# A one-core attention-and-MLP kernel with a written-out order: planner rates corrected and the order searched anew

## The chip, the cores and the metric

The kernel runs on one core of one Trainium2 chip. The engines that work here are TensorE (PE; its weight loads have a row of their own, PEld), VectorE (DVE), ScalarE (ACT), GpSimd (POOL) and SyncE (SP); DMA queues move data between HBM and the on-chip memories. The metric is the device time of one execution in microseconds (us), as the median of several runs. All times in the profile count from the first instruction of the profiled execution.

## The reference

The reference is a Nyström attention over 8 batches of 8 heads (576 tokens, head size 64, 32 landmarks), followed by a two-layer MLP with a squared ReLU on the 4608 tokens (model width 512, inner width 2048):

```python
q_lm = q.reshape(B, H, 32, 18, D).mean(axis=3); k_lm = likewise
A  = softmax(scale * q @ k_lm.T)      # 576 x 32 per head
Bm = softmax(scale * q_lm @ k_lm.T)   # 32 x 32
C  = softmax(scale * q_lm @ k.T)      # 32 x 576
Z  = Bm.T / (norm1(Bm) * norminf(Bm) + 1e-6)
for _ in range(6): Z = 2 * Z - Z @ Bm @ Z
x  = A @ Z @ C @ v                    # heads side by side: 4608 x 512
out = (relu(x @ w_in) ** 2) @ w_out
```

## The kernel before

The kernel never forms x. For each batch b it computes a matrix WP = Z C v w_in (128 x 2048 for each half of the heads), so that the first MLP layer is A·WP, and then relu, square and w_out.

Every piece of work is an `op` with a name, a table of engines that may run it with a planned duration for each, what it reads and writes, and a function that emits its instructions. An order written out by hand as one long string, `ORDER`, lists all 1437 ops. Each word is `name@banks/engine`: `@` gives the PSUM banks, `/A`, `/D`, `/P` choose ACT, DVE or POOL, and without a suffix the first engine of the op's table runs it. `Plan.schedule` walks the string once with the planned durations and transfer rates, gives each op a planned start, sorts by it, and the instructions are emitted in that order. So the string fixes, for each engine, a queue that is worked strictly from front to back: an instruction that waits holds up all that stand behind it on its engine.

The names, with b the batch:

- `ldk/ldq{b}.{r}`, `ldv{b}.{r}{i}`, `win{ch}{r}`, `wout{i}`: loads, all issued from POOL's DMA queue (fp32 in HBM, bf16 on chip). Two words that begin with `lx`: for batches 3 to 5 a second load of q or k into the tile `XS` for the landmarks (`load_xs`). `la{b}.{t}{j}`: for batches 6 and 7 three loads per operand (t = 0 is q, 1 is k), of which j = 1 and 2 *add* into the fp32 tile that j = 0 filled; that tile lies in `XS`, and each of the three waits for the one before it (`load_sums`, issued at line 443).
- Landmarks: `lm` (PE; batches 3 to 5 read `XS` at line 500), `lma` (line 510) and `lmc` (line 514) finish the sums of batches 6 and 7 in fp32 on DVE or POOL, `lme` scales, `lmt` transposes. `T{b}.{t}{r}`: DVE transposes of k and q.
- The 32 x 32 softmax: `B`, `Bmx`, `Bsb`, `Bex`, `Bsu`, `Brc`, `Bml`, and the norms `Bcs`, `Bnm`, `Bad` (line 670), `Brn`. The six steps of Z: `N{b}.{i}` on PE, `U{b}.{i}` on DVE, and from batch 2 on `bd{b}.{i}` (line 679, DVE or POOL) between them.
- The other softmaxes: `SS` or `SC`/`SA` on PE; `Cmx`, `Cex`, `Crc`, `Cnr` (line 422), `CT`; `At`, `Amx`, `Asb`, `Aex`, `Asu`, `Arc`, `Aml` (line 1081, in batches 0 and 1 line 1026), `Ap`, `Ab`.
- The product: `CV`, `CVe`, `Zm` (line 898), `ZC` (line 911, in batch 0 line 908), `ZCe`, `W` (line 935), `We`.
- The MLP: `F` (A·WP, four matmuls at line 1111), `R` (relu out of PSUM, ACT line 1132 or DVE line 1134), `Q` (square, ACT line 1139, DVE or POOL line 1141), `O` (w_out, four quarters of four matmuls each at line 1158 for each of 36 token tiles), `Oe` (copy out of PSUM), `St` (store, from SP's queue).

In the order the MLP of batch b stands between the small attention ops of batches b+1 and b+2, and `O` quarters fill PE where an attention chain would leave it waiting.

The planner counts two things that matter here. Ops that name DVE and POOL in `port=` are planned one after the other, as users of one port that the two engines share. A transfer lands after the bytes queued ahead of it, at a rate that depends on the planned time:

```python
sw = max(sw, free[e] + 0.5)
sw += o.nbytes / RATE["first" if sw < 23.0 else "then" if sw < 48.0 else "late"]
o.end, o.kind = sw + LAND, ""
```

The planned times set nothing on the chip except the order; on the chip an instruction starts when its semaphores and its engine allow it. A few short filler matmuls (line 1236) keep PE going in the first 22 us.

Of the kernel before, what the change touches and what calls it, by code (L numbers as in the profile page):

```python
# [265 lines left out]
def kernel(  # L266
# [207 lines left out]
    def attention(b):  # L474
# [32 lines left out]
        def landmarks_added():  # L507
            acc, ls, kS = ACC[i2], LS[:, 0, 0:256].rearrange("p (t r d) -> p t r d", t=2, d=D), ("LS", 0)
            for t in range(2):
                op(f"lma{b}.{t}", {"POOL": 0.9, "DVE": v_(384)}, lambda e, t=t: eng(e).tensor_tensor(  # L510
                    acc[:, t, :, 0:3], acc[:, t, :, 0:3], acc[:, t, :, 3:6], ALU.add),
                   R=[("ACC", i2, t)], W=[("ACC", i2, t)], port=("POOL", "DVE"))
# [765 lines left out]
c17 c0 ldk0.1 c1 ldq0.1 ldq0.0 ldk0.0 ldq1.0 ldk1.0 c2 ldk1.1 c12 c3 c5 ldq1.1 c6 c15 c13 ldv0.10  # L1278
T0.11 c10 c11 ldv0.11 lm0.1@0 c8 T0.01 lmc0.10/D ldv0.00 lmc0.11/D lme0.1 c9/A lmt0.1 T0.00
SC0.1@4 win31 lm0.0@1 Cmx0.1 T0.10 lme0.0 Cex0.1 lmt0.0 T1.00 bk0/P B0@6 c14/A Bmx0 SC0.0@4 Bsb0  # L1280
CT0.1 Bex0 win30 Bsu0 SA0.0@0 Brc0 Cmx0.0 Bml0/P Bce0@2 win10 Bmb0/A Bcs0 Btr0 Cex0.0 Amx0.0b
BBT0@3 Bnm0 Asb0.0b SA0.1@6 Brn0 CT0.0 Aex0.0b Zi0/P Yi0 win11 Amx0.0a N0.0@1 Amx0.1a lm1.0@5
win01 U0.0 Asu0.0b win00 N0.1@4 Asb0.0a lm1.0a U0.1 Aex0.0a ldv1.11 Amx0.1b N0.2@2 Arc0.0b
# [7 lines left out]
F0.12@4 R0.16 ldv1.00 F0.14@6 Zi1 Q0.22 c18 F0.10@2 Q0.18 R0.14 O1.0@1 Btr1 Q0.20 R0.10 ldv1.10
Q0.14 R0.12 F0.26@6 Q0.16 Aex1.0 F0.8@2 Q0.10 F0.30@4 R0.26/D R0.8 O0.0@0 T1.10 R0.30 ldq3.0
Q0.12/A F0.24@2 Asu1.0 Aex1.1 F0.28@6 T1.11 BBT1@4 lx3.1 R0.28 O1.1 Yi1 Asu1.1 Q0.8/A Q0.30/P
N1.0@5 O0.1 R0.24 U1.0 T2.10 ldk3.0 Q0.24/A N1.1@5 SC1.0@6,2 Q0.26 U1.1 O3.0@4 Cmx1.1 Arc1.0
N1.2@5 Cex1.1 O3.1 Aml1.0/P U1.2 Cmx1.0 N1.3@5 lm2.0@2 ldv3.11 U1.3 Q0.28 ldq3.1 Arc1.1 N1.4@5
Aml1.1/P lmc2.00 O1.2 U1.4 lmc2.01 Cex1.0 lme2.0 O0.2 lmt2.0 T2.00 lx3.0 B2@2 N1.5@5 O1.3 Bmx2
U1.5 Crc1 Bsb2 CT1.0 Bex2 O3.2 ldq5.0 Bsu2 Cmk1 Oe1.0 Brc2 CT1.1 Bml2 Ap1.1@6 St1 Btf2 ldk3.1
Btr2/A Bcs2 Zd1@3 CR1@1 Bct2 Ab1.1/A O3.3 bt2/D Bnm2 Bad2 CRe1 Brn2 T2.11 BBT2@5 Zi2/P CV1@6,1
Oe3.0 ldv2.10 Zm1 St3 O0.3 Yi2 CVe1.1/A CVe1.0 bd2.0 T2.01 ZC1@7 Ap1.0@2 Oe0.0/D ZCe1.0 N2.0@1
O2.0@4 Ab1.0/A ZCe1.1/D St0 U2.0 ldk4.1 bd2.1/D W1.2@5 W1.0@0 W1.1@2 We1.00 We1.01/D N2.1@7 O2.1  # L1300
We1.1 ldk5.0 U2.1 We1.2/D W1.3@0 ldv3.10 O2.2 We1.3 bd2.2 T3.00 F1.4@2 F1.0@6 R1.4/D F1.2@0 R1.0
N2.2@5 O2.3 Q1.4 R1.2 U2.2 bd2.3/D Q1.0/A F1.8@2 T3.10 Oe2.0 N2.3@7 F1.12@0 U2.3 F1.6@5 R1.8/D
St2 R1.12 lm3.0@4 bd2.4/D R1.6 Q1.12 Q1.2 F1.20@0 lme3.0 lx4.0 Q1.6 N2.4@6 lmt3.0 F1.10@2 R1.20
U2.4 ldv2.00 F1.14@4 T3.01 R1.10 B3@6 bd2.5 O5.0@0 R1.14 Bmx3 Bsb3 lx4.1 T3.11 Q1.10/A N2.5@3
SS2.0@6,1,4 Q1.20/A U2.5 ldq5.1 Q1.8 O5.1 At2.0 Q1.14/A ldv2.11 O5.2 Bex3 Bsu3 ldv3.00 Brc3
Amx2.0 SS2.1@4 O5.3 Bml3 Cmx2.1 ldq4.0 At2.1 O4.0@3 Cex2.1 Cmx2.0 O4.1 Oe5.0 ldk6.1 Asb2.0 Cex2.0
St5 F1.16@4 Zm2.2 Btf3 F1.18@1 Aex2.0 Bcs3 Amx2.1 F1.22@6 R1.16 O4.2 Asb2.1 R1.22 Q1.16/A F1.28@4
Q1.22 Bct3 F1.30@6 R1.18 R1.28/D O4.3 R1.30 Btr3 Crc2.0 Asu2.0 bt3 Q1.18/A F1.24@1 ldq6.0 Bnm3
F1.26@6 Bad3 R1.24 Brn3 Arc2.0 ldv4.00 O6.0@4 R1.26 Q1.24 Aml2.0 BBT3@5 Oe4.0 O6.1 ldv4.10 Aex2.1
Yi3 Q1.26 SS3.0@2,0,6 Q1.30/A Asu2.1 lm4.0@5 Zi3/P Q1.28/A At3.0 O6.2 Cnr2.0/A lx5.1 Crc2.1  # L1310
Arc2.1 Cnr2.1 lme4.0 O6.3 lx5.0 CT2.1 CT2.0 SS3.1@6 ldk5.1 Aml2.1 Oe6.0 O7.0@5 Cmx3.1 St6 bd3.0
O7.1 Cmx3.0 Cex3.1 At3.1 N3.0@4 O7.2 Cex3.0 U3.0 Zm2.1 lmt4.0 CV2@6,0 Ab2.1 bd3.1 Amx3.1 B4@2
ldk4.0 CVe2.0/A O7.3 Zm2.0 CVe2.1/A Crc3.1 Zm2.3 ldq4.1 Cnr3.1/A Bmx4 Ab2.0 N3.1@7 ZC2@4 O8.0@6
# [6 lines left out]
Zm3.0 R2.11 Arc3.1 O10.0@1 Q2.4 Q2.14/A Aml3.1 O10.1 R2.8 Asu3.0 Q2.8/A F2.15@2 lmt5.0 Arc3.0  # L1320
Q2.11/A CV3@4,6 Aml3.0 O9.1 Q2.13 CVe3.0/A CVe3.1/A Zm3.1 Ab3.0 R2.15 F2.12@4 T5.01 la6.10 ZC3@6
O9.2 R2.12 Q2.15 ZCe3.0/D Btr4/A la6.01 Q2.12/A O10.2 ZCe3.1/D bt4/D Bcs4 T4.00 W3.3@6 ldv6.11
W3.0@2 Ab3.1 W3.2@4 We3.0 We3.3/D O9.3 We3.2 O10.3 Oe9.0/D la7.10 BBT4@6 Bct4 F3.0@2 Oe10.0 Bnm4
F3.1@4 Bad4 Brn4 R3.0 T4.11 St10 Zi4/P O12.0@7 la7.01 R3.1 Yi4 bd4.0/D F3.2@0 T4.01 Q3.1/A St9
N4.0@6 W3.1@2 R3.2 U4.0 B5@4 O12.1 bd4.1/D We3.1 Bmx5 T5.00 N4.1@6 F3.3@0 Bsb5 Q3.2/A U4.1 O12.2
bd4.2 Bex5 R3.3/D Q3.0/A F3.6@4 Bsu5 la6.02 Brc5 T4.10 F3.5@0 N4.2@6 F3.4@2 Q3.3 R3.5 U4.2 la6.11
O12.3 R3.6 bd4.3/D Q3.5 R3.4 Bml5 N4.3@6 F3.9@0 Btf5 U4.3 Oe12.0 F3.7@4 Bcs5 bd4.4 R3.9/D F3.13@2
St12 la7.11 Bct5 F3.10@6 Q3.9/A R3.7/D N4.4@0 O11.0@1 R3.13 Q3.6 U4.4 R3.10 Bnm5 O11.1 T5.10
bd4.5 Q3.4/A SS4.0@2,4,6 Q3.7 Q3.10/A Bad5 N4.5@0 O11.2 la7.02 Brn5 Btr5 U4.5 At4.0 O11.3 bt5
Amx4.0 SS4.1@6 Zi5/P Oe11.0 ldv4.11 O13.0@0 Cmx4.1 St11 Cmx4.0 O15.0@1 Cex4.1 At4.1 O15.1 Cex4.0  # L1330
Asb4.0 BBT5@6 F3.12@4 Zm4.0 Aex4.0 Yi5 F3.11@2 Zm4.3 Crc4.1 Amx4.1 F3.8@6 R3.11 la6.12 Asu4.0
# [80 lines left out]
```

## Time and profile before

| What | Value |
|---|---|
| Median of 3 runs (lowest, highest) | 259.1 us (259.07, 259.11) |
| The profiled execution's own time | 259.34 us |
| Its span, first to last instruction | 257.6 us |
| Granted TensorE clock, mean | 0.999 |
| Busy: PE, DVE, ACT, POOL | 247.5, 212.5, 175.6, 85.1 us |
| Instructions | 7492 |
| HBM read, written | 48.50 MB, 9.44 MB |

In the profile a row of the timeline or of the chain gives a start, a length, the engine, the line of the source, the operation with its output and inputs, and a count. A bracket at the end of a timeline row is the time that the engine sat idle before it and what ended that idleness. A PE row's length runs to the modelled end of its last matmul, while the next group may start before that end, so a busy share of 96% doesn't say that PE runs at its peak; starts are compared with starts below. Rows of the 32 x 32 work and of POOL are rougher than the others.

### The profile page before, as it was taken

How to read it: one execution, taken by the hardware profiler on the slowest of the kernel's cores; microseconds unless marked ns; L12 is line 12 of the kernel's file. 1: busy time of each engine (PE TensorE's matmuls, PEld its weight loads, DVE VectorE, ACT ScalarE, POOL GpSimd, SP SyncE). 2: the span in 40 equal slices, each digit the busy share in tenths (PEclk: the TensorE clock that was granted, in tenths of full speed). 3: DMA queues.
4: the chain of work that ended last, by engine and by line, in shares of the span. 5: the costliest groups of instructions: out<-in, count | busy, mean ns of one | idle time of the engine just before them, and what ended most of it. 6: DMA issues, size and time to landing. Idle time of an engine off the chain costs nothing.

```text
span 257.6 us, 7492 instructions
## 1 busy us (share of the span) xinstructions
PE 247.5 (96%) x3043; PEld 138.1 (54%) x3043; DVE 212.5 (82%) x553; ACT 175.6 (68%) x324; POOL 85.1 (33%) x137
## 2 busy tenths in 40 slices
...
GB/s 99 209 190 204 206 209 207 208 240 227 224 225 209 223 230 283 164 194 181 196 138 205 192 156 94 3 80 46 43 21 104 43 42 0 3 124 42 10 67 129
DMA packets 24610, 36.53 MB, mean 142 GB/s; under 512 B 2560, under 2 KB 13632, under 8 KB 24576
## 3 DMA queue, kind: packets, MB, share of 16 engines
...
q1 hardware_dynamic: 5760, 9.31, 14.0%
q8 instruction: 24, 0.39, 0.6%
q10 hardware_dynamic: 160, 0.13, 0.2%
...
HBM read 48.50 MB, written 9.44 MB: 225 GB/s over the span
## 4 chain that ended last, share of the span: by engine, by line
PE 66%; DMA 15%; DVE 10%; POOL 3%; issue 2%; ACT 2%; DVEq 0%; POOLq 0%
PE ps L1158 38%; PE ps L1111 16%; DMA X<-in_q_dram 9%; DMA XS<-in_q_dram 6%; PE ps L935 3%; DVE RS L1134 2%; PE ps L864 2%; DVE G L1141 2%; POOL X L429 1%; PE ps L778 1%; ACT WP L416 1%; DVE sm L816 1%; PE ps L529 1%; PE ps L742 1%; DVE An L1081 1%
## 5 line engine op out<-in xcount | busy, mean ns | idle before, releaser
L1158 PE MATMUL ps<-w_out,G 128*128 128x512 bf16 (+1 forms) x592 | 138.3, 374 | 0.3 <-DVE RS L1134 0.3
L1158 PEld LDWEIGHTS <-G 128*128 128x128 bf16 x592 | 53.2, 98 | 53.9 <-issue 6.0
L1111 PE MATMUL ps<-AT,WP 128*128 128x288 bf16 (+2 forms) x512 | 71.2, 286 | 1.1 <-DVE RS L1134 0.8
L1132 ACT ACTIVATE RS<-ps 128x576 bf16<-128x576 f32 (+2 forms) x101 | 61.1, 651 | 10.5 <-PE ps L1111 5.0
L1111 PEld LDWEIGHTS <-WP 128*128 128x128 bf16 x512 | 48.5, 98 | 20.6 <-issue 2.5
L1139 ACT ACTIVATE G<-RS 128x576 bf16<-128x576 bf16 (+2 forms) x55 | 36.4, 686 | 2.1 <-DVE RS L1134 1.8
L416 ACT COPY OS<-ps 128x512 f32<-128x512 f32 (+1 forms) x32 | 18.3, 573 | 23.0 <-PE ps L1158 21.8
L1141 DVE TENSOR_TENSOR G<-RS 128x576 bf16<-128x576 bf16 (+2 forms) x71 | 30.1, 445 | 2.6 <-ACT RS L1132 2.0
L416 ACT CAST WP<-ps 128x1024 bf16<-128x1024 f32 (+1 forms) x25 | 23.5, 983 | 6.7 <-PE ps L935 6.5
L679 POOL TENSOR_TENSOR BD<-ST,blkb 128x256 bf16<-128x256 bf16 x15 | 10.8, 718 | 47.4 <-DVE ST L756 43.2
L1134 DVE TENSOR_SCALAR RS<-ps 128x576 bf16<-128x576 f32 (+2 forms) x27 | 20.4, 760 | 4.9 <-PE ps L1111 3.8
L484 DVE STREAM_TRANSPOSE TT<-X 128x576 uint32<-128x576 uint32 x32 | 24.3, 761 | 0.0
L819 ACT ACTIVATE C<-ps,sm 128x576 bf16<-128x576 f32 x16 | 14.2, 902 | 7.7 <-DVE sm L816 7.7
L756 DVE SCALAR_TENSOR_TENSOR ST<-ST,ps 128x128 bf16<-128x128 bf16 (+1 forms) x48 | 12.8, 266 | 5.9 <-PE ps L742 3.6
L455 POOL DMA_DIRECT2D V<-in_v_dram x24 | 14.5, 603 | 6.2 <-DMA X<-in_q_dram 2.6
L420 DVE COPY OS<-ps 128x512 f32<-128x512 f32 x5 | 3.4, 675 | 12.3 <-PE ps L1158 12.3
L816 DVE TENSOR_REDUCE sm<-ps 128x1 f32<-128x576 f32 x16 | 11.5, 747 | 1.2 <-PE ps L778 1.1
L1236 PE MATMUL ps<-onesb 128*128 128x512 bf16 (+1 forms) x36 | 10.6, 392 | 1.6 <-DVE onesb L352 1.6
L420 DVE CAST WP<-ps 128x1024 bf16<-128x1024 f32 (+1 forms) x9 | 9.9, 1100 | 1.8 <-PE ps L935 1.7
L429 POOL DMA_DIRECT2D X<-in_q_dram x16 | 9.8, 642 | 4.1 <-PE ps L1111 2.2
L429 POOL DMA_DIRECT2D X<-in_k_dram x16 | 9.7, 607 | 3.6 <-DMA X<-in_k_dram 1.3
L1081 DVE TENSOR_TENSOR An<-SA,smA 128x640 bf16<-128x640 f32 (+1 forms) x12 | 10.3, 864 | 0.1
...
## 6 DMA issues: line engine op xcount, KB each, us to landing
...
X<-in_q_dram POOLq DMA_DIRECT2D x16, 288.0 KB, 11.0
...
XS<-in_q_dram POOLq DMA_DIRECT2D x6, 384.0 KB, 6.5
XS<-in_k_dram POOLq DMA_DIRECT2D x6, 384.0 KB, 7.1
...
```

Source lines behind the costliest of these rows:

```text
L416: nc.scalar.copy(o, i)
L429: lambda e: nc.gpsimd.dma_start(x[:, t, r].rearrange("p s d -> p (s d)"), src),
L455: lambda e, r=r, p0=p0, n=n, src=src: nc.gpsimd.dma_start(vv[32 * p0:32 * (p0 + n), r].rearrange("p s d -> p (s d)"), src),
L484: op(f"T{b}.{t}{r}", {"DVE": v_(576) + 0.02}, lambda e, r=r: nc.vector.transpose(tt[:, t, r].rearrange("p s m e -> p (s m e)").bitcast(U32 ...
L816: op(f"Cmx{b}.{r}", {"DVE": v_(576)}, lambda e, r=r: nc.vector.tensor_reduce(s_[:, 12 + r:13 + r], cbanks(r), axis=AX.XY, op=ALU.max, nega ...
L819: op(f"Cex{b}.{r}", {"ACT": a_(576) + 0.27}, lambda e, r=r: nc.scalar.activation(Cs[r][:].rearrange("p x u -> p u x"), cbanks(r), AF.Exp, ...
L1111: nc.tensor.matmul(ps[:, ph.at + i, 0:w], lhsT=wp[:, r, 128 * ff:128 * ff + 128], rhs=at[:, r, t0:t0 + w], start=(r == 0), stop=(r == 1))
L1132: nc.scalar.activation(rs, pair(ph, w), AF.Relu)
L1134: nc.vector.tensor_scalar(out=rs, in0=pair(ph, w), scalar1=0.0, scalar2=None, op0=ALU.max)
L1139: nc.scalar.activation(g, rs, AF.Square)
L1141: eng(e).tensor_tensor(g, rs, rs, ALU.mult)
L1158: nc.tensor.matmul(bank(po)[:, 0:c1 - c0], lhsT=G[:, f, lo:lo + P], rhs=w_out[:, f, c0:c1], start=(f == 0), stop=(f == NF - 1))
```

## The change

Four planner constants are corrected: the rate of late loads goes from 0.385 to 0.355 MB/us, the counted size of an adding load from 1.5 to 0.5 of 786,432 bytes, and POOL's planned durations for the fp32 additions from 0.9 to 1.5 us (`lma`) and from 0.65 to 1.0 us (`lmc`). None of the four is seen by the chip. `ORDER` is replaced as a whole: the same 1437 ops, each emitted as before, in another order, with other PSUM banks, and 164 of them on another engine: 67 go from DVE to ACT, 62 from ACT to DVE, 20 from POOL to DVE, 14 from DVE to POOL and one from POOL to ACT. PE's ops, the loads and the stores keep their engines.

```diff
-RATE = {"sw": 0.375e6, "hw": 0.2e6, "first": 0.385e6, "then": 0.4e6, "late": 0.385e6}
+RATE = {"sw": 0.375e6, "hw": 0.2e6, "first": 0.385e6, "then": 0.4e6, "late": 0.355e6}
...
-                op(f"lma{b}.{t}", {"POOL": 0.9, "DVE": v_(384)}, lambda e, t=t: eng(e).tensor_tensor(
+                op(f"lma{b}.{t}", {"POOL": 1.5, "DVE": v_(384)}, lambda e, t=t: eng(e).tensor_tensor(
...
-                op(f"lmc{b}.0{j}", {"DVE": v_(256), "POOL": 0.65}, lambda e, j=j: eng(e).tensor_tensor(
+                op(f"lmc{b}.0{j}", {"DVE": v_(256), "POOL": 1.0}, lambda e, j=j: eng(e).tensor_tensor(
...
-ADD_COST = 1.5
+ADD_COST = 0.5
```

The order, at the places that the prediction speaks of. The end of batch 0's attention and the first `F`:

```diff
-N0.3@2 win20 lme1.0 U0.3 Cmk0 CVe0.1/A lmt1.0 CVe0.0/A N0.4@6 Aml0.0a/P T1.01 CR0@5 B1@0 CRe0/A
-wout0 U0.4 Bmx1 bk1 N0.5@4 Bsb1 Ap0.0@5 U0.5 Asu0.1a ldq2.1 Zd0@3 Ab0.0/A SA1.0@0 Zm0 Bex1
-Arc0.1b Bsu1 Aml0.1b/P ZC0@2 Brc1 Amx1.0 SA1.1@6 ZCe0 c7 Arc0.1a Bml1/P Asb1.0 Aml0.1a/P W0.1@2
-Amx1.1 W0.3@4 wout1 We0.1 Ap0.1@0 Bmb1 Asb1.1 ldk2.1 We0.3 ldk2.0 F0.6@2 Ab0.1 W0.0@6 Blo1/P R0.6
...
-R0.20/D R0.2 F0.18@4 R0.0 Q0.2 W0.2@6 Bad1 F0.22@2 R0.18/D We0.2 Q0.0/P F0.16@0 Brn1 R0.22/D
...
+CT0.0 c7 N0.1@1 Asb0.0a lm1.0a U0.1 Aex0.0a Amx0.1b N0.2@0 Asu0.0a lm1.0b U0.2 Arc0.0a T1.01
+Aml0.0a/P N0.3@4 lme1.0 CV0@5,0 U0.3 win31 Asb0.1b N0.4@7 lmt1.0 Aex0.1b win30 Crc0 U0.4 CVe0.0/A
+Cmk0 Asu0.1b CVe0.1/A N0.5@7 bk1/P CR0@5 U0.5 Amx0.1a CRe0/A Zd0@6 Asu0.0b wout0 Arc0.1b Arc0.0b
+Zm0 SA1.0@4 Aml0.0b wout1 Asb0.1a ZC0@7 Ap0.0@5 Amx1.0 ZCe0 ldk2.0 Aex0.1a W0.0@0 Ab0.0/A Asu0.1a
+ldq2.0 We0.00 W0.1@2 Arc0.1a We0.01/D Aml0.1b/P SA1.1@6 We0.1 Asb1.0 Aml0.1a/P B1@0 Amx1.1 Aex1.0
+F0.4@2 ldk2.1 Ap0.1@4 Bmx1 ldq2.1 R0.4 Bsb1 Asb1.1 Bex1 F0.2@0 Ab0.1/A Q0.4 W0.2@2 R0.2/D F0.6@6
+We0.2 F0.20@4 Bsu1 Q0.2/P R0.6/D F0.0@0 R0.20 W0.3@2 wout2 R0.0/D F0.18@6 We0.3 Q0.20 F0.22@4
```

The adding loads of batches 6 and 7, and what stands around them:

```diff
-lm5.0@1 R2.9 Q2.0 Q2.6/A N3.4@0 F2.4@6 Q2.9 la6.00 U3.4 F2.13@4 R2.10 bd3.5/D CT3.0 O9.0@0 lme5.0
...
-ldv6.00 Q3.15/A N5.2@6 ldq7.1 CV4@2,4 Zm4.2 O14.3 CVe4.0/A CVe4.1 Ab4.0 ZC4@2 U5.2 O15.3 Oe14.0
-bd5.3/D Aml4.1 ZCe4.0 N5.3@3 O13.3 Oe15.0 ZCe4.1/D U5.3 T5.11 St15 W4.0@6 Oe13.0 W4.1@1 Ab4.1
-O16.0@3 We4.1 bd5.4/D T6.00 St13 lma7.0 O16.1 We4.0 lma6.0/D W4.2@1 St14 W4.3@4 We4.2/D F4.0@6
...
+lm5.0@4 R2.5 St6 Q2.0 Q2.5/A R2.6/D N3.4@5 F2.9@0 la7.00 lme5.0 F2.7@2 U3.4 R2.9 St7 bd3.5/D
+F2.8@6 Bsu4 lmt5.0 Q2.6/A la6.00 Asb3.0 N3.5@5 F2.4@0 R2.7 O10.0@4 Brc4 Bml4 R2.4 U3.5 Zm3.0
...
+Q2.11/A Q2.10 CT3.1 B5@6 R2.13 F2.14@0 la7.01 Bmx5 Btr4 Bsb5 O9.1 Q2.8/A T4.01 Aex3.0 Bcs4 bt4
+CV3@2,6 Bct4 R2.14 Bnm4 la6.01 Asu3.0 O9.2 CVe3.0/A CVe3.1/A Bad4 Brn4 Q2.14/A Zm3.2 F2.15@2
+Aml3.1 ldq5.1 ZC3@0 F2.12@6 la6.10 T4.10 R2.15 O10.1 ZCe3.0 Arc3.0 Q2.15/A ZCe3.1/D Q2.13 O10.2
+R2.12 Aml3.0 Q2.12/A W3.2@2 Ab3.1 W3.0@6 Bex5 W3.3@0 We3.2/D la6.02 We3.0 O9.3 We3.3 O10.3 Ab3.0
+ldq4.0 T4.11 la7.10 BBT4@6 Oe9.0 F3.3@2 Oe10.0/D O12.0@7 R3.3 Yi4 St10 Zi4/P la7.02 Q3.3/A W3.1@0
+bd4.0/D F3.1@5 T5.10 We3.1 St9 N4.0@4 O12.1 ldq7.1 lma6.0/D R3.1 la6.11 U4.0 Bsu5 Q3.1/A Brc5
+bd4.1/D F3.0@3 F3.2@0 ldv6.11 T4.00 R3.0 N4.1@2 F3.6@5 R3.2 U4.1 O12.2 bd4.2/D Q3.0/A Q3.2 N4.2@4
...
+W4.2@6 ldq7.0 Aml4.0 W4.0@4 O16.0@1 We4.0 Ab4.1 Ab4.0 O16.1 We4.1 lma7.0/D We4.2/D F4.0@4 lme6.0
+lma7.1 O16.2 R4.0 lmt6.0 T6.11 O16.3 lmc7.00/P N5.5@0 lmc7.01/P SS5.0@6,4,2 Oe16.0 U5.5 Q4.0/A
```

Of the ops that move between engines, by kind: 17 `R` and 25 `Q` go from DVE to ACT, 21 `R` and 18 `Q` from ACT to DVE; of POOL's, `lma7.0`, `bd7.4`, nine more `bd`, `bt3`, `bt5` and seven other small ones go to DVE, and `Q0.0` to ACT; to POOL go `bk1`, `Q0.2`, `lmc7.01`, six `bd`, `bt4` and four other small ones. The second load of `XS` for batch 5 (`lx5.0`) has 33.31 MB of loads up to and with it in POOL's queue in place of 34.78 MB (fp32 bytes, an adding load with its real 0.39 MB; `ldk6.1`, `ldq6.0` and others go behind it, `ldk6.0` and others ahead), and `la6.00` 36.31 in place of 37.54 MB.

171 lines of the change are left out of this document (81 added, 90 removed).

## The prediction

> **What bounds the kernel now.** I read the page first, then the chain, then PE's timeline wherever PE sat idle, then the engines that it had waited for, last the loads.
>
> ```profile
> span 257.6 us, 7492 instructions
> PE 247.5 (96%) x3043; PEld 138.1 (54%) x3043; DVE 212.5 (82%) x553; ACT 175.6 (68%) x324; POOL 85.1 (33%) x137
> ...
> PE 66%; DMA 15%; DVE 10%; POOL 3%; issue 2%; ACT 2%; DVEq 0%; POOLq 0%
> ...
> L1132 ACT ACTIVATE RS<-ps 128x576 bf16<-128x576 f32 (+2 forms) x101 | 61.1, 651 | 10.5 <-PE ps L1111 5.0
> ...
> L1139 ACT ACTIVATE G<-RS 128x576 bf16<-128x576 bf16 (+2 forms) x55 | 36.4, 686 | 2.1 <-DVE RS L1134 1.8
> ...
> L1141 DVE TENSOR_TENSOR G<-RS 128x576 bf16<-128x576 bf16 (+2 forms) x71 | 30.1, 445 | 2.6 <-ACT RS L1132 2.0
> ...
> L1134 DVE TENSOR_SCALAR RS<-ps 128x576 bf16<-128x576 f32 (+2 forms) x27 | 20.4, 760 | 4.9 <-PE ps L1111 3.8
> ```
>
> PE is the bound: it carries most of the chain, and no other engine is near its span. The chain in order of time gives the two phases and the length of dense groups.
>
> ```profile
> 16.83 0.81 PE ps L529 x6
> ...
> 24.13 0.44 DVE ZM L890
> ...
> 24.82 0.47 issue
> ...
> 52.67 0.97 PE ps L1158 x4
> 53.75 0.49 PE ps L1037 x4
> 54.30 0.86 PE ps L1158 x4
> ...
> 99.31 0.49 PE ps L1111 x4
> ```
>
> Up to the first `F` the chain changes engine at each step; later it is nearly all PE. A quarter of `O` takes 0.86 when its like follows and 0.97 when another shape of matmul does, so a change of shape costs about 0.1 us. PE's timeline shows the first `F`, the stalls behind it, and the place of `N4.0`:
>
> ```profile
> 27.84 0.61 PE L1111 MATMUL ps<-AT,WP 128*128 128x256 bf16 x4 [0.21 <-ACT WP L416]
> ...
> 33.73 1.03 PE L1111 MATMUL ps<-AT,WP 128*128 128x256 bf16 x8 [0.83 <-DVE RS L1134]
> ...
> 96.46 0.73 PE L500 MATMUL ps<-XS,seg 96*32 96x256 bf16 x20 [0.75 <-DMA XS<-in_q_dram]
> ...
> 111.95 0.23 PE L742 MATMUL ps<-ST,BD 128*128 128x64 bf16 x2
> ...
> 135.25 1.04 PE L1158 MATMUL ps<-w_out,G 128*128 128x512 bf16 x4
> 136.45 0.22 PE L911 MATMUL ps<-ZM,CV 128*128 128x64 bf16 x2 [0.17 <-DVE ZM L898]
> 136.91 0.23 PE L911 MATMUL ps<-ZM,CV 128*128 128x64 bf16 x2 [0.24 <-DVE CV L420]
> ...
> 209.08 1.02 PE L1158 MATMUL ps<-w_out,G 128*128 128x512 bf16 x4 [0.25 <-DVE RS L1134]
> ```
>
> A quarter's row is 1.04 long here and 0.86 in the chain: 0.17 of a row's tail would lie under the next group, so an idle time in brackets understates the loss by that much. With it the stalls are 1.00, 0.82 (0.92 less the 0.1 for the change of shape), 0.75 (0.34 and 0.41) and 0.42, together 2.99 us. Other stalls behind the first `F` are 0.1 to 0.4 each, some 1.4 us in all by my comparison of starts.
>
> **The causes of the stalls**, in DVE's timeline, then POOL's, then the usual length of two of the lines:
>
> ```profile
> 31.82 1.13 DVE L670 TENSOR_SCALAR sm<-sm 128x2 f32<-128x2 f32 x1
> ...
> 133.69 1.69 DVE L1081 TENSOR_TENSOR An<-SA,smA 128x640 bf16<-128x640 f32 x1
> 135.40 0.99 DVE L898 TENSOR_TENSOR ZM<-ST,blk 64x128 bf16<-64x128 bf16 x1
> ...
> 205.64 0.78 DVE L422 TENSOR_SCALAR C<-C,sm 128x576 bf16<-128x576 bf16 x1
> ```
>
> ```profile
> 31.86 1.05 POOL L1141 TENSOR_TENSOR G<-RS 128x512 bf16<-128x512 bf16 x1
> ...
> 134.79 1.51 POOL L510 TENSOR_TENSOR XS<-XS 128x384 f32<-128x384 f32 x1
> ...
> 205.37 0.88 POOL L679 TENSOR_TENSOR BD<-ST,blkb 128x256 bf16<-128x256 bf16 x1 [0.85 <-DVE sm L830]
> ```
>
> ```profile
> L898 DVE TENSOR_TENSOR ZM<-ST,blk 64x128 bf16<-64x128 bf16 x24 | 6.0, 251 | 0.5
> L422 DVE TENSOR_SCALAR C<-C,sm 128x576 bf16<-128x576 bf16 x8 | 3.4, 419 | 0.1
> L510 DVE TENSOR_TENSOR XS<-XS 128x384 f32<-128x384 f32 x2 | 1.1, 532 | 0.0
> ```
>
> Three times a DVE op is far longer than its like while a POOL op runs beside it: `Bad1` beside `Q0.0`, `Aml4.0` and `Zm4.2` beside `lma7.0`, `Cnr7.1` beside `bd7.4`. In the old order each of these POOL words stands behind the DVE word that it met, so the plan kept them apart; but its semaphores were satisfied earlier, and POOL ran it at once. The fourth stall is `lm5.0` waiting for the `XS` load.
>
> **The change, part by part.** The four constants cost nothing themselves; the order is what is paid.
>
> *Engine moves.* `R`: DVE gains 21 and loses 17, so DVE +4 x 0.76 = +3.0 and ACT -2.6. `Q`: ACT gains 25 and loses 18, so ACT +7 x 0.69 = +4.8 and DVE -3.1. Sums: DVE 0, ACT +2, with 45 and 82 us idle. POOL gains 14 ops and loses 21; its load issues come no later for that. All this lies beside PE's work: 0. Were that cover gone at one `F`, it would cost what 33.73 shows, 1 us. SP keeps its stores, and the tail (`O35`, `Oe35.0`, its stores) is as before: 0.
>
> *Up to the first `F`.* `lm1.0` at 16.83 waits for the eighth load, and the first eight loads are issued in the same order, so everything to there: 0. Behind it `Bmx1`, `bk1`, `Bsb1`, `Asu0.1a` and `Asb0.1a` leave DVE's queue ahead of `Zm0`, and `T1.01` goes where PE is in `lm1.0b` and `CV0`; `Amx0.1a`, `Asu0.0b` and small ones come in. I take `Zm0` 0.8 sooner than 24.13. `B1` and `Ap0.0` no longer stand ahead of `ZC0` either, but ACT then has `Aex0.1a` and `Ab0.0` before the two `We` that `F0.4` needs. First `F` at 27.1 instead of 27.84: -0.74 (bounds: 0, if the 0.47 of "issue" falls on `W0.1`, and -1.2). In exchange `Ap0.1` (0.6, by the 0.49 of its like with four matmuls, and two more) goes behind the first `F`, and the new order has 120 changes of shape, the old 117 (+0.3). Net +0.2.
>
> *`Bad1`, `ZC4`, `O28`.* `Q0.0` is on ACT; `Q0.2`, now POOL's, meets on DVE only `R`s, which read PSUM, before `Q0.20`. `lma7.0` and `bd7.4` are on DVE. -1.00 - 0.75 - 0.42 = -2.17. Late next: POOL words whose release lies ahead of a DVE word of the port. I counted them: ten in the old order, three of which cost those 2.17, five in the new (`bk1`, `Bml5`, `lmc6.01`, `lma7.1`, `bd6.4`). The worst is `lma7.1`: it's free to run behind `ldq7.0`'s issue, beside `Aml4.0` and `lma7.0` on DVE, in front of `We4.2` and so of `SS5.0`'s bank. Bounds 0 and 2.17; five in ten would be 1.1, but four of them are short. I take +0.5.
>
> *`lm5.0`'s load.* What the loads' queue moved, how long adding loads took, and POOL's wait for one:
>
> ```profile
> q0 software_dynamic: 7698, 9.56, 105.3%
> ```
>
> ```profile
> DMA to landing us min/median/max: 5.0/7.0/7.8
> ```
>
> ```profile
> XS<-in_q_dram POOLq DMA_DIRECT2D x1, 384.0 KB, 5.2
> ```
>
> ```profile
> XS<-in_k_dram POOLq DMA_DIRECT2D x1, 384.0 KB, 5.1
> ```
>
> ```profile
> 105.16 1.23 POOL L443 DMA_DIRECT2D XS<-in_q_dram  x1 [4.78 <-DMA XS<-in_q_dram]
> ```
>
> The first row is the window 45 to 97: 9.56 MB as bf16 is 19.1 MB of fp32, 0.368 MB/us. `lx5.0` has 34.78 - 33.31 = 1.47 MB less ahead of it, so it lands 4.0 sooner, at 92.5. PE reaches `lm5.0` at 96.46 - 0.82 - 0.74 - 1.00, less three `F`s that went behind it (1.5), plus `Ap0.1` and a change of shape (0.7): 93.1. It doesn't wait: -0.82 (bounds -0.82 and -0.3, as 2% of rate over 46 us is 0.9). Other loads are closer than before: `lx4.1`, 7.81 MB ahead of the old `lx5.0`, lands at 75.2 where `lm4.0` is due at about 75. I take +0.2 (0 to 0.7).
>
> *The adding loads.* They were far from any use before; now `lma6.0/D` stands on DVE between `N4.0` and `U4.0`, and everything on DVE queues behind its wait. `la6.00` landed by 105.16, when POOL went on to `la6.01`; with 37.54 - 36.31 = 1.23 MB less ahead that is 101.8. Two legs, each waiting for the last, at 5.2 and 5.1 (issued in the windows 105 to 105.5 and 131.5 to 132.5, little ahead of them) end at 112.1. `N4.0` was at 111.95; less 0.74, 1.00 and 0.82, plus 0.9 for PE work moved ahead of it and 0.2 from above, it comes at 110.5. PE then has `O12.1`, `F3.0`, `F3.2` (1.9) before `N4.1`, which needs `lma6.0` (0.53), `U4.0`, `Bsu5`, `Brc5`, `bd4.1` (about 1.2 with their handovers): `lma6.0` may begin at 110.7 and begins at 112.1. With `ldq4.0` for `T4.00` right behind, issued after `la6.02`, I take +1.3. Bounds: 0, and with both legs at the median of 7.0, +4.8. I choose the short legs because the queue has drained by then.
>
> The Trainium skill (DMA: Bandwidth & Descriptors, Anatomy of one DMA) gives 2.0 us and the bytes at 436 GB/s for such a transfer, 2.9 for 393,216 bytes. By it the legs, with their 1.23 of issue, would take 4.1, `lma6.0` would wait for nothing, and the sum would be 257.0; the trace's shortest, 5.0, disagrees.
>
> *Sum*: +0.2 - 2.17 + 0.5 - 0.82 + 0.2 + 1.3 = -0.8. The profiled execution took 259.34, its span 257.6; that gives 258.5, and as the median of the runs, 259.1, lies 0.24 below, **258.3**.
>
> **The rivals.** *Quick legs*: the adding loads land in time, -1.3: 257.0. For it: drained queues; against it: no leg under 5.0. Chance 0.2. *Slow legs*, the other side: at 7.0 the wait before `U4.0` grows by 3.5 to 4.8, and the time is 261.8; from 5.6 a leg on, the gain is gone. For it: 7.0 is the median, and stores and `ldq5.1` share the queue; against it: the long ones had loads ahead. Chance 0.13. *Collisions come back*, so that the new order doesn't do what it's said to: `lma7.1` and one more POOL word cost what three did, 2.17 in place of 0.5: 260.0. For it: POOL runs a word when released, as all three cases show; against it: half as many candidates. Chance 0.2. The Trainium skill (SBUF — State Buffer, Who interferes with whom) lets whichever starts first hold the shared port for its whole instruction, and names DVE ops with two SBUF inputs; by that `lma7.1` would hold `lma7.0` for up to its own length. The DVE rows of 1.13 and 0.99 above agree.
>
> **How the numbers follow.** My forecast has 0.47, with a range of its own of 257.3 to 259.3. A measurement of this kernel can tell about 0.2% (0.5 us). Faster by more: 0.47 x 0.72 + 0.2 x 0.95 + 0.2 x 0.1 = 0.55; within: 0.17; slower: 0.28. The range that holds the time 8 times in 10 leaves out the slow legs and the far end of the quick ones: 256.3 to 260.2.
>
> **What would show it.** Right: `L670`, `L898` and `L422` on DVE near their usual lengths, PE's wait for `XS` gone, first `F` near 27.1, DVE idle before `L510` some 1.4 near 112 and PE's `L742` behind it waiting for `L756` or `L679`. Wrong: PE idle in new places behind lengthened DVE rows, above all at 136 to 141, PE waiting for a load before 80, or first `F` no sooner.

## The result, and the profile after

The kernel after the change takes **268.0 us** (median of 4 runs, 265.2 to 268.8); the kernel before took 259.1 on the same chip (259.07 to 259.61). The ratio is 1.0315, with a 95% interval of 1.0278 to 1.0352. In a later comparison, among the experiments below, it was 266.3 against 259.3, ratio 1.0253 (1.0229 to 1.0276). The prediction was 258.3 with a range of 256.3 to 260.2; it was wrong: the time lies 9.7 above the forecast and 7.8 above the range, on the other side of the kernel before.

The profiled execution took 268.76, the slowest of its four. Its page, in the rows for the span, the engines' busy time, PE's granted clock in 40 slices, and the chain:

```profile
span 267.1 us, 7488 instructions
...
PE 252.6 (95%) x3046; PEld 139.4 (52%) x3046; DVE 215.1 (81%) x554; ACT 180.5 (68%) x330; POOL 81.1 (30%) x130
...
PEclk9999999999999999979979999999999999999999
...
PE 69%; DMA 13%; DVE 9%; POOL 3%; issue 3%; ACT 1%; POOLq 0%
```

No engine has become the bound. What is new are two slices with a clock of 7 tenths, the 18th and the 21st, which is 113.5 to 120.2 and 133.5 to 140.2 us. PE's timeline of the kernel after, around the places that the prediction spoke of:

```profile
22.79 0.58 PE L850 MATMUL ps<-CMX,cpick 128*128 128x8 f32 x4 [1.02 <-DVE CMX L843]
28.06 0.61 PE L1111 MATMUL ps<-AT,WP 128*128 128x256 bf16 x4 [0.17 <-ACT WP L416]
...
94.60 0.84 PE L500 MATMUL ps<-XS,seg 96*32 96x256 bf16 x24
...
115.50 1.60 PE L1111 MATMUL ps<-AT,WP 128*128 128x288 bf16 x7 [1.97 <-DVE ST L756]
...
117.03 1.15 PE L1111 MATMUL ps<-AT,WP 128*128 128x288 bf16 x4
117.97 1.64 PE L1158 MATMUL ps<-w_out,G 128*128 128x512 bf16 x4
...
132.32 0.23 PE L742 MATMUL ps<-ST,BD 128*128 128x64 bf16 x2 [2.50 <-DVE BD L679]
132.39 1.46 PE L1158 MATMUL ps<-w_out,G 128*128 128x512 bf16 x4
...
134.47 1.89 PE L1158 MATMUL ps<-w_out,G 128*128 128x512 bf16 x4
...
139.68 1.67 PE L1158 MATMUL ps<-w_out,G 128*128 128x512 bf16 x7 [0.96 <-DVE ST L756]
```

The first `F` comes at 28.06, not at 27.1: PE's `CR0` (L850) waited 1.02 for DVE's `Cmk0`. `lm5.0` (94.60) no longer waits for its load. Then PE stands twice, 1.97 and 2.50 us, and behind both stands the same four matmuls of `O` (L1158) take 1.64, 1.46 and 1.89 where they took 1.03. The waits come from DVE. Its timeline:

```profile
21.35 1.30 DVE L843 TENSOR_TENSOR CMX<-cmk,sm 128x16 f32<-128x16 f32 x1
...
114.70 0.56 DVE L510 TENSOR_TENSOR XS<-XS 128x384 f32<-128x384 f32 x1 [2.53 <-DMA XS<-in_q_dram]
...
118.28 0.78 DVE L484 STREAM_TRANSPOSE TT<-X 128x576 uint32<-128x576 uint32 x1 [2.31 <-DMA X<-in_q_dram]
...
119.26 0.29 DVE L679 TENSOR_TENSOR BD<-ST,blkb 128x256 bf16<-128x256 bf16 x1
...
131.51 0.56 DVE L510 TENSOR_TENSOR XS<-XS 128x384 f32<-128x384 f32 x1 [2.83 <-DMA XS<-in_k_dram]
...
137.37 1.23 DVE L898 TENSOR_TENSOR ZM<-ST,blk 64x128 bf16<-64x128 bf16 x1
...
148.03 2.25 DVE L1081 TENSOR_TENSOR An<-SA,smA 128x640 bf16<-128x640 f32 x1
```

`lma6.0` (114.70) and `lma6.1` (131.51) are the first additions on the sums of batch 6, each at the head of DVE's queue and each waiting for the last adding load of its chain; between them `T4.00` (118.28) waits for `ldq4.0`, issued behind that chain, and `bd4.2` (119.26), which PE's `N4.2` needs, comes behind it. `Cmk0`, `Zm4.1` and `Aml4.0` are long, at 1.30, 1.23 and 2.25. POOL's timeline has what ran beside those three, and the issues of the chains:

```profile
21.45 1.16 POOL L990 TENSOR_TENSOR BK<-LT,blkw 128x512 bf16<-128x512 bf16 x1
...
102.46 1.21 POOL L443 DMA_DIRECT2D XS<-in_q_dram  x1
...
109.39 1.25 POOL L443 DMA_DIRECT2D XS<-in_q_dram  x1 [4.37 <-issue]
...
126.10 1.23 POOL L443 DMA_DIRECT2D XS<-in_k_dram  x1 [5.19 <-DMA XS<-in_k_dram]
...
137.30 1.21 POOL L514 TENSOR_TENSOR LS<-LS,XS 128x256 f32<-128x256 f32 x1
...
148.52 1.02 POOL L510 TENSOR_TENSOR XS<-XS 128x384 f32<-128x384 f32 x1
```

`bk1`, `lmc6.01` and `lma7.1` are the companions, three of the five words that the prediction had counted. `la6.01` was issued at 102.46, `la6.02` at 109.39, `la6.12` at 126.10; the view of DMA issues gives 5.9, 5.2 and 5.4 us from there to landing, so they land at 108.4, 114.6 and 131.5, and with the last two the chains of q and k end.

Put beside PE's dense work in both traces, start by start, the 9.44 us by which PE's last `O` comes later split up as follows. The two groups of stalls for adding loads, from `F3.2` to `N4.2` and from `N5.1` to `N5.2`, are 3.90 and 4.17, together **8.07**. The collisions of `lmc6.01` and `lma7.1` are 1.13 before `N5.4` and 0.84 before `F4.0`, together 1.97. The first `F` is 0.22 later, and PE has 0.88 more to do behind it (`Ap0.1`, changes of shape). Small stalls grow by 1.26 in all; that is what remains of the 9.44, and no single cause is shown for it. Gone are `Bad1` 0.99, `lm5.0` 0.81, the two behind `ZC4` 0.75 and the one behind `Cnr7.1` 0.41, together 2.96.

### The profile page after: what moved, and what is told of

Its sections match the earlier page's. It is cut to its first block, busy times and chain, and to the rows that moved or that the text cites. A ratio compares the mean times of both kernels' runs of the same rounds, so it can differ in the third digit from the quotient of the medians.

```text
span 267.1 us, 7488 instructions
## 1 busy us (share of the span) xinstructions
PE 252.6 (95%) x3046; PEld 139.4 (52%) x3046; DVE 215.1 (81%) x554; ACT 180.5 (68%) x330; POOL 81.1 (30%) x130
## 3 DMA queue, kind: packets, MB, share of 16 engines
HBM read 48.50 MB, written 9.44 MB: 217 GB/s over the span
## 4 chain that ended last, share of the span: by engine, by line
PE 69%; DMA 13%; DVE 9%; POOL 3%; issue 3%; ACT 1%; POOLq 0%
PE ps L1158 39%; PE ps L1111 18%; DMA XS<-in_k_dram 7%; DMA X<-in_q_dram 4%; PE ps L935 3%; DMA XS<-in_q_dram 2%; POOL X L429 2%; PE ps L778 2%; PE ps L864 2%; DVE An L1081 1%; PE ps L1236 1%; POOL XS L443 1%; ACT RS L1132 1%; DVE SA L1071 1%; PE ps L529 1%
## 5 line engine op out<-in xcount | busy, mean ns | idle before, releaser
L1158 PE MATMUL ps<-w_out,G 128*128 128x512 bf16 (+1 forms) x592 | 140.8, 377 | 1.3 <-DVE ST L756 1.0
L1158 PEld LDWEIGHTS <-G 128*128 128x128 bf16 x592 | 54.1, 98 | 56.7 <-issue 8.6
L1111 PE MATMUL ps<-AT,WP 128*128 128x288 bf16 (+2 forms) x512 | 74.5, 289 | 2.9 <-DVE ST L756 2.0
L1139 ACT ACTIVATE G<-RS 128x576 bf16<-128x576 bf16 (+2 forms) x63 | 42.0, 688 | 0.8 <-DVE RS L1134 0.2
L1141 DVE TENSOR_TENSOR G<-RS 128x576 bf16<-128x576 bf16 (+2 forms) x63 | 26.9, 443 | 5.4 <-ACT RS L1132 4.5
L416 ACT COPY OS<-ps 128x512 f32<-128x512 f32 (+1 forms) x29 | 16.5, 571 | 20.3 <-PE ps L1158 19.1
L1134 DVE TENSOR_SCALAR RS<-ps 128x576 bf16<-128x576 f32 (+2 forms) x31 | 23.1, 748 | 5.6 <-PE ps L1111 4.2
L679 POOL TENSOR_TENSOR BD<-ST,blkb 128x256 bf16<-128x256 bf16 x11 | 7.7, 703 | 52.1 <-DVE ST L756 52.1
L455 POOL DMA_DIRECT2D V<-in_v_dram x24 | 16.4, 706 | 4.8 <-PE ps L864 2.4
L420 DVE COPY OS<-ps 128x512 f32<-128x512 f32 x8 | 5.5, 685 | 8.4 <-PE ps L1158 8.2
L742 PEld LDWEIGHTS <-BD 128*128 128x128 bf16 x72 | 6.5, 100 | 9.6 <-DVE BD L679 4.0
```

The source lines that it names most:

```text
L416: nc.scalar.copy(o, i)
L455: lambda e, r=r, p0=p0, n=n, src=src: nc.gpsimd.dma_start(vv[32 * p0:32 * (p0 + n), r].rearrange("p s d -> p (s d)"), src),
L1111: nc.tensor.matmul(ps[:, ph.at + i, 0:w], lhsT=wp[:, r, 128 * ff:128 * ff + 128], rhs=at[:, r, t0:t0 + w], start=(r == 0), stop=(r == 1))
L1134: nc.vector.tensor_scalar(out=rs, in0=pair(ph, w), scalar1=0.0, scalar2=None, op0=ALU.max)
L1139: nc.scalar.activation(g, rs, AF.Square)
L1141: eng(e).tensor_tensor(g, rs, rs, ALU.mult)
```

## The experiments: where the waits stand

My theory when I had read this trace was that two words at the head of DVE's queue cost most of the loss (**DVE**). The rival was that POOL's own short words, which stand behind issues that wait for landings, hold PE as much, and come into view when DVE doesn't (**POOL**). The first kernel moves only the additions:

```diff
-N4.0@4 O12.1 ldq7.1 lma6.0/D R3.1 la6.11 U4.0
+N4.0@4 O12.1 ldq7.1 R3.1 la6.11 U4.0
...
-O16.1 We4.1 lma7.0/D We4.2/D
+O16.1 We4.1 lma6.0/D lma6.1/D lmc6.00 lmc6.01/P lma7.0/D We4.2/D
```

> Only the first and second additions of batch 6's sums (lma6.0, lma6.1, lmc6.00, lmc6.01) move, to just before lma7.0 in the order; the loads stay where they are. In the kernel after, lma6.0 stands 2.53 us on DVE at 114.70 and lma6.1 2.83 us at 131.51, each for an adding load. Theory DVE (the loss is these two waits at the head of DVE's queue, with what follows them on PE): the second group of PE stalls (2.66 + 0.43 + 0.25 + 0.82 = 4.2 us from 132.3 to 136.2) goes; the first one stays, because T4.00, four words further on, waits for ldq4.0, which lands at 118.25 as before: 263.8 us. Rival POOL (POOL's own compute words bd5.2, bd5.4, bd5.5 stand behind issues that wait for an adding load to land, so the wait only changes engine): bd5.2 can't start before the issue of ldk7.0 ends at 131.9, nor bd5.4 before that of la7.12 at 137.2; some 2 to 3 us are gained: 265.5. Rival rest-of-order (the loss is spread elsewhere): 268.

Measured: 263.8 us, ratio to before 1.0195 (1.0174 to 1.0217). The kernel after didn't run beside this one and the next two; its own ratios were 1.0315 and 1.0253. The second group of stalls is gone; the first is there, before `N4.2`, since DVE now waits 2.98 us for `T4.00`'s load. This is what DVE said. POOL stood in the way only a little in this execution: `la6.12`, which waits for `la6.11` to land, was issued at 124.44, 1.7 us sooner than in the kernel after, PE didn't wait for `bd5.2`, and it waited 0.95 us for a later word of POOL, at 137.61.

The second kernel gives `T4.00` its load in time as well:

```diff
-la6.02 We3.0 O9.3 We3.3 O10.3 Ab3.0 ldq4.0 T4.11 la7.10
+la6.02 We3.0 O9.3 We3.3 O10.3 Ab3.0 T4.11 la7.10
...
-Bsu4 lmt5.0 Q2.6/A la6.00 Asb3.0
+Bsu4 lmt5.0 Q2.6/A la6.00 ldq4.0 Asb3.0
```

> As e1_sums_later, and ldq4.0 is issued right behind la6.00 (at some 97.5) instead of behind la6.02 (110.14), so that T4.00 finds its data by about 104. Theory DVE: both groups of stalls go, 3.9 + 4.2 us: 260 us. Rival POOL: the first group goes (3.9), and of the second what remains behind POOL's issues grows by as much, since POOL's issues wait for landings that come at the same time as before: 265 us, PE waiting for BD (L679) of a POOL word at about 132 and again at about 138. Rival rest-of-order: 268.

Measured: 265.9 us, ratio 1.0273 (1.023 to 1.0317): no better than the kernel after in its second comparison, and 6 us from what DVE said. PE's and POOL's timelines of this kernel:

```profile
134.15 0.29 PE L742 MATMUL ps<-ST,BD 128*128 128x64 bf16 x2 [4.84 <-POOL BD L679]
```

```profile
127.61 1.23 POOL L443 DMA_DIRECT2D XS<-in_k_dram  x1 [9.52 <-DMA XS<-in_k_dram]
...
132.39 1.71 POOL L679 TENSOR_TENSOR BD<-ST,blkb 128x256 bf16<-128x256 bf16 x1
```

POOL stood 9.52 us with `la6.12`, which waits for `la6.11` to land; `bd5.2` stands behind it and seven more issues, and PE waited 4.84 for it. With DVE's waits gone the same landing holds PE through POOL. DVE alone falls, and POOL holds. The third kernel takes POOL's short words out of that queue:

```diff
-Zi4/P Bml5/P bd4.3 bd5.2 bd5.4 bd5.5
+Zi4 Bml5 bd4.3/D bd5.2/D bd5.4/D bd5.5/D
```

> As e3_sums_later_q4_earlier, and six short compute words (Zi4, Bml5, bd4.3, bd5.2, bd5.4, bd5.5) go from POOL to DVE, so that none of PE's work between 105 and 145 stands behind an issue of POOL. Both theories, DVE and POOL: 260 us (268.0 - 3.9 - 4.2), and the difference to e3 is the price of POOL's queue: nothing by DVE, 5 us by POOL. If it isn't below 263, something else than these two queues binds between 110 and 140. PE's granted clock in 110 to 120 and 130 to 140 returns from 0.83 to above 0.95.

Measured: 263.5 us, ratio 1.0184 (1.015 to 1.0218). Between 110 and 142 PE has no stall above 0.2 left, as both said, but the time is 3.5 above what they gave. The wait has moved again. ACT's and PE's timelines:

```profile
145.47 0.42 ACT L418 ACTIVATE LM<-LS 128x256 bf16<-128x256 f32 x1 [4.72 <-POOL LS L514]
```

```profile
146.48 0.28 PE L778 MATMUL ps<-TT,LT 32*32 32x288 bf16 x1 [3.06 <-ACT RS L1132]
```

`lmc6.01`, left on POOL, now stands behind `la7.12`, which waited 6.93 us for a landing, and behind the loads that follow it; ACT stands 4.72 with `lme6.0`, and PE 3.06 for ACT. So every word that shares a queue with these landings, or waits for one that does, is a place where the loss can stand. The fourth kernel takes them all away, `bk1` too:

```diff
-bk1/P lmc6.01/P lma7.1 lmc7.00/P lmc7.01/P
+bk1 lmc6.01 lma7.1/D lmc7.00 lmc7.01
...
-N6.3@6 lme7.0 O18.3
+N6.3@6 lma7.1/D lmc7.00 lmc7.01 lme7.0 O18.3
```

> As e6_and_pool_words_on_dve, and the words that stalled PE there or in the kernel after beside GpSimd leave POOL: bk1, lmc6.01, lma7.1, lmc7.00 and lmc7.01 go to DVE, the last three to just before lme7.0, long after la7.12 has landed. Theory (waits at the heads of DVE's and POOL's queues and four collisions are the whole difference, 8.9 us): the stall of 3.21 before SS5.1 and the 2.3 that follow it go, and Cmk0's 1.1 ahead of the first F: 263.5 - 5.5 - 1.0 = 257.0, below both kernels; Cmk0 at 0.2, first F at 27.1. Rival (the order of after is worse in other places too, or DVE becomes the bound with its added work): 260 to 262.

Measured: 259.7 us, ratio 1.0012 (0.9998 to 1.0026): all but 0.1% of the loss is back, yet not the 257.0. The first `F` comes at 27.10 with `Cmk0` at its usual length. The stall of 3.06 is gone, but PE's timeline has idle times of 0.71 before `SS5.0`, 0.39 before `SS5.1` and 0.34 before the `O` behind it, each behind DVE, and 0.51 before `W5.1`, behind ACT. DVE has eleven more words in this kernel, so the rival may have part of it; but the kernel after has the third of these waits too (0.4), and that the added words are the reason isn't shown.

## The experiments: why the data are late

That the waits stand at landings doesn't say why the landings are late. In the kernel after, and then in the kernel before, I made the twelve loads plain copies (the first of each chain is one anyway), so that the sums of batches 6 and 7 are left out:

```diff
-                    accum_op=ALU.add if j else ALU.bypass),
+                    accum_op=ALU.bypass),
```

> The kernel after with the twelve loads of the sums of batches 6 and 7 all plain copies: the second and third of each chain overwrite in place of adding, so the landmarks of these two batches are wrong; bytes, destinations, order and waits are as before. Theory queue (an adding load holds the queue for longer than a plain one of its bytes, so chains and whatever is queued behind them land late): legs of la6.01 and la6.02 below 4.5 us in place of 5.9 and 5.2, ldq4.0 lands by 115 and la6.12 by 126 in place of 118.25 and 131.5, and the time falls by 3 to 6 us, to 262 to 265. Rival latency (the legs are as long for plain loads, and what costs is that each waits for the last to land): legs as before, 268.

> The kernel before with the twelve loads of the sums of batches 6 and 7 all plain copies, so that the landmarks of these two batches are wrong; everything else as it is. Theory (adding loads are as slow in the old order as in the new, but there nothing stands close behind them): la6.01 and la6.02 take some 3.5 us in place of 5.2 and 5.0 where the queue is short, la7.12 lands 4 us or more sooner, and the time doesn't change: 258.5 to 259.5. Rival (plain loads are simply a faster program, whatever the order): 5 us less or more, as in g1_plain_loads.

Measured for the kernel after: **259.0 us**, ratio 0.9985 (0.9968 to 1.0002). One argument of one call takes the whole loss away. Measured for the kernel before: 258.9, ratio also 0.9985 (0.9969 to 1.0002): nothing changes there. So an adding load is slow in both orders, and only the new one makes somebody wait for it. The latency rival falls. The views of DMA issues, from issue to landing, of the kernel after with adding loads (`la6.01`, `la6.12`), with plain ones (the same two), and of the kernel before with plain ones (`la6.01`, `la6.02`):

```profile
XS<-in_q_dram POOLq DMA_DIRECT2D x1, 384.0 KB, 5.9
...
XS<-in_k_dram POOLq DMA_DIRECT2D x1, 384.0 KB, 5.4
```

```profile
XS<-in_q_dram POOLq DMA_DIRECT2D x1, 384.0 KB, 3.5
...
XS<-in_k_dram POOLq DMA_DIRECT2D x1, 384.0 KB, 3.8
```

```profile
XS<-in_q_dram POOLq DMA_DIRECT2D x1, 384.0 KB, 4.0
...
XS<-in_q_dram POOLq DMA_DIRECT2D x1, 384.0 KB, 3.6
```

Some 1.6 to 2.4 us are the addition's in the new order. In the old order `la6.01` and `la6.02` took 5.2 and 5.0 in the kernel before, which makes it 1.2 and 1.4. A queue that holds adding loads also moves less. What the loads' queue moved from 110 to 120 and from 120 to 130 (packets, MB, share), first with adding loads, then with plain ones:

```profile
q0 software_dynamic: 728, 1.41, 78.4%
...
q0 software_dynamic: 718, 1.13, 67.0%
```

```profile
q0 software_dynamic: 713, 1.98, 79.0%
...
q0 software_dynamic: 766, 1.89, 86.5%
```

About as many packets, but 2.54 MB in place of 3.87. Part of that is a queue that stands empty for longer; by the shares it moved 1.75 MB in 10 us of full work in place of 2.34, a quarter less. The packets of 102 to 103 point to the reason, in the counts by size: 47 packets of adding loads are all under 2 KB, 15 of plain ones, with the same bytes, are all above.

```profile
DMA packets 47, 0.07 MB, mean 72 GB/s; under 512 B 0, under 2 KB 47, under 8 KB 47
```

```profile
DMA packets 15, 0.07 MB, mean 69 GB/s; under 512 B 0, under 2 KB 0, under 8 KB 15
```

By the fit of the Trainium skill (DMA: Bandwidth & Descriptors, Anatomy of one DMA) a transfer of 393,216 bytes takes 2.9 us, as an estimate. The plain loads, at 3.5 to 4.0, come near it; for adding loads, at 4.9 and more in every trace here, it is too short by some 2.0 or more.

## The experiment on the clock

In the trace after, the `O`s behind the two stands are long. Is that PE's clock, or do the loads slow PE down? I filled most of each stand with matmuls that nobody reads:

```diff
+    for name, n in (("x0", 8), ("x1", 10)):
+        xb = Bank(1, "x")
+        op(name, {"PE": pe(512, n)}, lambda e, n=n, xb=xb: [nc.tensor.matmul(
+            ps[:, xb.at, :], lhsT=onesb[:, 0:P], rhs=onesb[:], start=True, stop=True) for _ in range(n)],
+           R=["onesb"], W=[xb], alloc=[xb], ni=2 * n)
...
-F3.0@3
+x0@6 F3.0@3
...
-N5.1@2
+x1@3 N5.1@2
```

> The kernel after, with 8 matmuls of 128x512 ahead of F3.0 and 10 ahead of N5.1, of constants into a free PSUM bank, read by nobody: PE works (1.7 and 2.15 us) through most of the two waits, which themselves stay. Theory clock (part of the loss isn't waiting, but PE at about half speed for some 3.4 us behind each idle stretch: O12.2's four matmuls take 1.64 instead of 1.03, O14.1's 1.89): 1.6 us less behind each wait, less 0.2 for a matmul that comes late: 265.2 us, O12.2 and O14.1 at 1.03, clock above 0.95 in 110 to 120 and 130 to 140. Rival (the rows are long for another reason, such as the loads on SBUF): 268 to 268.5, rows as long as before.

The windows of the kernel after (110 to 120, 130 to 140; the granted clock is the third number from the end), and then of this kernel, followed by rows of its PE timeline:

```profile
110.00:120.00 10.00, 7.91 (x49) 3.95 (x47) 4.99 (x15) 5.44 (x9) 6.11 (x9) 0.83 0.94 193
...
130.00:140.00 10.00, 6.72 (x88) 2.41 (x89) 6.66 (x14) 2.87 (x5) 5.42 (x9) 0.83 1.12 210
```

```profile
110.00:120.00 10.00, 9.79 (x69) 5.31 (x69) 5.98 (x18) 7.16 (x12) 6.50 (x10) 1.00 0.99 209
...
130.00:140.00 10.00, 8.54 (x106) 3.48 (x105) 9.29 (x23) 5.86 (x11) 4.98 (x8) 1.00 1.09 203
```

```profile
113.53 1.89 PE L1233 MATMUL ps<-onesb 128*128 128x512 bf16 x8 [0.19 <-ACT RS L1132]
...
116.48 0.65 PE L1111 MATMUL ps<-AT,WP 128*128 128x288 bf16 x4
116.97 1.03 PE L1158 MATMUL ps<-w_out,G 128*128 128x512 bf16 x4
...
132.52 1.04 PE L1158 MATMUL ps<-w_out,G 128*128 128x512 bf16 x4
```

The clock is 1.00 with as busy a DMA share, and the rows are back at 1.03 and 0.65: it is the clock, and PE's idleness has a part in it. The four runs of this kernel have mean clocks of 0.998 to 1.000, the nine of the kernel after 0.985 to 0.997. But a stand doesn't bring it on each time. This is a stand, and the window behind it, in the kernel with three words moved to DVE that is described in the next section:

```profile
129.33 0.23 PE L742 MATMUL ps<-ST,BD 128*128 128x64 bf16 x2 [2.50 <-DVE BD L679]
```

```profile
130.00:140.00 10.00, 9.37 (x174) 4.35 (x176) 9.62 (x23) 6.32 (x13) 3.86 (x5) 1.00 1.11 223
```

The stand is as long as the second of the kernel after, and the clock stays at 1.00. The second profile of the kernel after, from the next section, has 1.00 behind a stand of 1.87 and 0.83 behind one of 2.05. What decides isn't shown.

In the kernel after, the rows at 117.03, 117.97, 132.39 and 134.47 together are 2.4 us longer than these, but not all of that is lost. Behind the first stand PE would have waited anyway: `N4.2` (119.61) needs `bd4.2`, which ends on DVE at 119.55. In the second profile the clock is 1.00 there, PE waits 1.10 for `bd4.2`, and it takes 2.67 us from `N4.1` to `N4.2` against 2.71. Behind the second stand it takes 3.83 from `N5.1` to `N5.2`, where the kernel with the filled stands takes 2.36. So some 1.5 of the 8.07 is a slow clock and not waiting. The total doesn't show it cleanly: 265.7 us, ratio 1.0281 (1.0248 to 1.0315), between the two ratios of the kernel after.

## The experiments on collisions, and the kernel after once more

> The kernel after once more, unchanged, on the chip of the three runs beside it, because its own runs spread from 265.2 to 268.8. Theory (the two waits for adding loads hang on landings, which vary from run to run by a microsecond or two, where the kernel before hangs on PE): the median lies between 266 and 268.5, and the landing of la6.12 that the profile shows goes with its span: 131.5 in the profile of 268.8. Rival (one disturbed measurement): all runs within 0.5 us of each other.

Measured: 266.3 us (265.4 to 266.6), ratio 1.0253 (1.0229 to 1.0276). The profile has a span of 264.7, and `la6.12` lands at 130.15 where it landed at 131.48 in the span of 267.1: 1.3 of the 2.4 us between the two spans are this landing's. On the same chip, with `bk1`, `lmc6.01` and `lma7.1` on DVE:

```diff
-bk1/P lmc6.01/P lma7.1
+bk1 lmc6.01 lma7.1/D
```

> The kernel after with three words from POOL to DVE in their old places: bk1, lmc6.01, lma7.1. Theory (collisions on the port cost Cmk0 1.1 us ahead of the first F, Zm4.1 1.1 at 137 and Aml4.0 1.45 at 148, of which PE lost 1.0, 1.1 and 0.8): Cmk0, Zm4.1 and Aml4.0 at 0.2, 0.2 and 0.8, first F at 27.1, and 2 to 3 us less than a0_after_again. Rival (what is gained ahead of a landing is lost again in the wait for it, as b1_before_no_collisions showed for Bad1 and lm5.0, and lma7.1 on DVE waits for la7.12): 0.5 to 1.5 us less.

Measured: 264.3 us, ratio 1.0172 (1.014 to 1.0203), which is 2.0 us below the kernel after. DVE's and PE's timelines:

```profile
21.24 0.17 DVE L843 TENSOR_TENSOR CMX<-cmk,sm 128x16 f32<-128x16 f32 x1
```

```profile
27.18 0.61 PE L1111 MATMUL ps<-AT,WP 128*128 128x256 bf16 x4 [0.17 <-ACT WP L416]
```

`Cmk0` takes 0.17, and the first `F` comes at 27.18, 0.87 sooner. `Zm4.1` and `Aml4.0` are no longer long. Two thirds of the 2.99 that PE lost to the three in the kernel after are gained; at most one third is swallowed by the waits for landings.

## The experiments on the stalls that the change removes

The other half of the prediction, that four stalls of the old order cost 3 us, can be tried in the old order itself.

```diff
-Q0.0/P
+Q0.0/A
...
-lma7.0
+lma7.0/D
...
-bd7.4
+bd7.4/D
```

> The kernel before with three words on another engine and nothing else: Q0.0 on ACT, lma7.0 on DVE, bd7.4 on DVE, in their old places in the order. Theory (the term of -2.17 in the prediction: three DVE instructions were long because a GpSimd instruction ran beside them, and PE waited for them): 256.9 us, L670 of batch 1 at 0.2 in place of 1.13, Aml4.0 at 0.8 in place of 1.69, Cnr7.1 at 0.36 in place of 0.78. Rival (the stalls are made up elsewhere, or ACT and DVE pay for the added words): 258.5 to 259.

Measured: 258.1 us, ratio 0.996 (0.9945 to 0.9976): 1.0 to 1.4 us, not 2.2. All three stalls are gone, but PE's timeline has this:

```profile
61.70 0.84 PE L500 MATMUL ps<-XS,seg 96*32 96x256 bf16 x24 [0.32 <-DMA XS<-in_q_dram]
...
96.41 0.84 PE L500 MATMUL ps<-XS,seg 96*32 96x256 bf16 x24 [0.81 <-DMA XS<-in_q_dram]
```

`lm5.0` was at 96.46 before and is at 96.41: it waits for a landing, and what PE gains ahead of that is lost there, `Bad1`'s 0.99 whole. Only the 1.17 of `lma7.0` and `bd7.4` counts. The next two kernels bring the loads forward, first `lx5.0`'s, then `lx3.0`'s, and put `ldk6.1` and `ldq6.0` first behind `lx5.0` (shown here), then behind `bd3.0`, the last word of the long line; `lx3.0` goes from behind `lmt2.0 T2.00` to just ahead of `ldq3.1`:

```diff
-O4.1 Oe5.0 ldk6.1 Asb2.0
+O4.1 Oe5.0 Asb2.0
...
-Q1.18/A F1.24@1 ldq6.0 Bnm3
+Q1.18/A F1.24@1 Bnm3
...
-O6.3 lx5.0 CT2.1 CT2.0 SS3.1@6 ldk5.1 Aml2.1 Oe6.0 O7.0@5 Cmx3.1 St6 bd3.0
+O6.3 lx5.0 ldk6.1 ldq6.0 CT2.1 CT2.0 SS3.1@6 ldk5.1 Aml2.1 Oe6.0 O7.0@5 Cmx3.1 St6 bd3.0
```

> As b1_before_no_collisions, and ldk6.1 and ldq6.0, which batch 6 needs some 60 us later, are issued behind lx5.0 instead of ahead of it: 1.18 MB less stand before lx5.0, which lands 3 us sooner. Theory (the term of -0.82: lm5.0 waits only for that load): 256.1 us, PE's 0.75 of waiting for XS near 96 gone. Rival (the adding loads, which share the queue from 97 on, lose what lx5.0 gains): as b1, 256.9.

> b2_and_lm5_load_earlier with what was late next there: lx3.0 is issued ahead of ldq3.1 (lm3.0 waited 0.86 for it at 61.7), and ldk6.1 and ldq6.0 come behind bd3.0 in POOL's order instead of ahead of it (N3.0 waited for bd3.0 at 83.5, 0.4). Theory (each of these waits stands alone on PE's path): 257.7 - 0.9 - 0.4 = 256.4, PE without idle time above 0.5 us between the first F and 200. Rival (the next load, lx4.1 or lx5.0, takes the gain): 257.2 to 257.7.

Measured: 257.7 (ratio 0.9942, 0.9922 to 0.9962) and 257.3 (0.9916, 0.99 to 0.9932). The medians fall at each step, but by less than its own wait, and neighbouring intervals overlap; only the two steps together are clear of noise. In the first, `lm3.0` waits 0.86 at 61.70 as it did at the same moment above, and takes what was gained before it. In the second neither waits:

```profile
61.02 0.84 PE L500 MATMUL ps<-XS,seg 96*32 96x256 bf16 x24
...
95.32 0.84 PE L500 MATMUL ps<-XS,seg 96*32 96x256 bf16 x24
```

The stalls behind the first `F` are 2.24 us in all, against 4.62 in the kernel before and 12.96 in the kernel after. That kernel is the fastest of this study, 2.0 us below the kernel before on its chip, with six words changed.

## Why the prediction was wrong

- *The adding loads* (+1.3, bounds 0 to 4.8) failed, and decided the result: 8.07. **First**, the landing of `la6.02`. `la6.00` landed at 101.9, as predicted (101.8). Then I let POOL go on at once and gave each leg 5.2 and 5.1 "because the queue has drained by then". It hadn't: `la7.01`, `ldq5.1` and `la6.10` were in it, `la6.01` took 5.9, POOL issued it 0.5 late behind `la7.01` and `bt4` and issued `la6.02` 1.0 after the landing. The chain ended at 114.6 instead of 112.1, and `ldq4.0` behind it at 118.25. **Second**, and larger, the sum has one chain and there are two: I never worked out `la6.10` to `la6.12` for `lma6.1`, and DVE waited 2.83 us for it, PE 4.17 with what followed. **Third**, I costed a stand of PE at its length; some 1.5 us more came by the clock. That the words on POOL and ACT would have stood there next, the second and the third kernel showed.
- *The slow legs* rival had this mechanism, at 261.8. Its legs of 7.0 were too long for the first chain, its count of one chain too short. Its 5.6 us for a leg, from which the gain is gone, was the mean of the two measured, 5.6. The median of 7.0 that stood for it counts the four first loads of the chains, which are plain copies; the eight that add have a median of 6.3 in the kernel before.
- *The quick legs* rival was tried by the plain loads: 259.0 and not 257.0. For the 2.0 between them the next two points are enough, 0.96 and 1.47 in the kernel after.
- *The first `F` at 27.1* failed at one word: `bk1` leaving DVE's queue was counted as a gain, but on POOL it ran beside `Cmk0` and PE lost 1.02. Without that collision it came at 27.10 and 27.18 in two kernels, so the rest of this step fits.
- *New collisions* (+0.5) was too small. Among the five candidates, called short but for `lma7.1`, three met a DVE word with two inputs from SBUF: 1.02 before the first `F`, 1.13 for `lmc6.01`, 0.84 for `lma7.1`. That is 2.99, or 1.97 behind the first `F`; taking all three away gained 2.0. The rival *collisions come back* had 2.17, but left the adding loads at 1.3.
- *Removed stalls* (-2.17 and -0.82) were right in the trace after: -2.15 and -0.81. They added up there because `lx5.0` also lands sooner, at 90.4; the first kernel in the old order shows that there they don't.
- *More work behind the first `F`* (+0.6 and +0.3) was right, at 0.88. *Tight loads* (+0.2): PE has no wait for a load between the first `F` and 110. *Engine moves* at nothing isn't settled: the 1.26 of small stalls may hold some of it.
